# First pair's outputs from direct scores between its blocks; second pair's keys turned on TensorE

## Chip, cores and metric

One core of a Trainium2 chip. The metric is device time in microseconds (us), the median of three runs. Names of engines as in the profile: PE (TensorE, with PEld for its weight loads), DVE (VectorE), ACT (ScalarE), POOL (GpSimd), SP (SyncE, which issues the DMAs).

## What is computed

Attention with a decaying state, then two gated layers, in float32 and better (weights come as 64-bit numbers). Cut to what matters:

```python
# r, k, v, w: (4, 8, 768, 48); u: (8, 48)
for t in range(S):
    cur = einsum("bhd,bhe->bhde", u[None] * kt, vt)
    y[:, :, t] = einsum("bhd,bhde->bhe", rt, state + cur)
    state = wt[:, :, :, None] * state + einsum("bhd,bhe->bhde", kt, vt)
x = y.transpose(0, 2, 1, 3).reshape(3072, 384)
x = (1 / (1 + exp(-(x @ w_gate))) * (x @ w_val)) @ w_out         # 384 -> 1536 -> 384
h = x @ w_in                                                     # 384 -> 2048 -> 384
out = (h * tanh(log1p(exp(h)))) @ w_out2
```

## The kernel before

The sequence of 768 is cut into 24 blocks of 32 (`C`), taken in 12 pairs; block `e` (0 or 1) of pair `p` is block `2p+e`. One pair gives 256 rows of x, and each pair goes through the same stages.

*Attention of a pair.* `fine` builds the scores inside small squares of a block from products of r and k rows (`pt`, `blk`, mostly POOL) that DVE sums into `A`. `coarse` transposes r, k, w on DVE into `RD`, `KD`, `WD`, scales `RD`, and makes the scores further from the diagonal on PE (`scores`, tile `lp`, one bank per block). DVE transposes `A` into `X`, and twelve small copies per block merge `lp` into `X` (`merge`, L715). `keys` multiplies the keys by decays on POOL, transposes them on DVE (`flip`, tile `KT`, L782), and ACT copies the parts into `KK` (`gather`, L797; eight copies for a pair below 2). `states_apart` multiplies `KK` by v on PE (`kp`, L902), and DVE adds the product to the decayed state (`s`, L913, L915; the decay is L833). `rows_out` multiplies `X` by v and `RD` by the old state on PE (`yp`, L948); ACT and DVE copy the sums as a high and a low fp16 half (`xs`, L976, L979). For the first two pairs `turn` transposes `xs` on PE against an identity (`xp`, L1000), and ACT and DVE copy one half each to `xt`; later pairs use transposing DMAs. For pairs 0 and 1 the order is: outputs of block 0, state behind block 0, outputs of block 1, state behind block 1. So block 1 of pair 0 waits for the state behind block 0.

*The first layer.* `gate` runs 24 rounds of nine products for each pair (`gv`, L1072) from `xt` and the two weights `wgs`, `wvs`; ACT takes the sigmoid, DVE the product (L1088), and both split it into `gt`. `out1` multiplies by `wos` (`o`, L1140). Beside the gates of pair 0 the weights are decoded from 64-bit numbers: SP loads a chunk into one of three raw buffers, ACT makes two parts (`word`, `low`), DVE joins them (L350, L444), ACT casts the high half, and DVE or POOL subtracts the low one (L364, L457). The second layer (`h`, L1250; `o`, L1365) follows, and its products come after the attention.

*What sets the order.* Every step is a task with the engines it may go to, a cost, and keys that it reads and writes. `Plan.run` gives each task a due time, counted back from the end, plays the program once with the costs, and issues the instructions in the order that results; a task with two engines goes to the one that the play finds free. So a change of a cost or of an order in the code moves instructions on all engines. An engine then works through its own list in order. `FIRST` is the pair of gate steps before which the two halves of the next pair's tail (`tail1`, `tail2`) are entered; `MERGE` says which blocks ACT merges; for pairs below `TURNED`, `turn_keys` transposes the keys on PE instead of DVE; none did.

Of the kernel before, what the change touches and what calls it, by code (L numbers as in the profile page):

```python
# [8 lines left out]
F32 = mybir.dt.float32  # L9
# [4 lines left out]
ALU = mybir.AluOpType  # L14
# [28 lines left out]
YPOS = (4, 7)  # L43
FIRST = (9, 11)
LATE = 3
# [6 lines left out]
APART = 2  # L52
TURNED = 0
KBANKS = ((('pg', 0), ('pg', 1)), (('at', 0), ('at', 2)))
# [8 lines left out]
WORDS = 256  # L63
MERGE = lambda p, e: e == 0 or p == 0
CROWD = 208
# [149 lines left out]
def mixer_moe_kernel(  # L215
# [266 lines left out]
    late = {}  # L482
    yps = {}
    kps = {}
    xss = {}
# [155 lines left out]
    def coarse(p, cells):  # L641
# [85 lines left out]
        parts = [(*RD, n) for n in range(3)]  # L727
        attn("pe", BURST, scores, [*parts, KD], banks, burst=space(p), words=256)
        attn("dve", 1.9, flip_a, [*cells], X[0] + X[1])
        for e in range(2):  # L730
            for n in range(4):
                on = {"act": 0.85} if MERGE(p, e) else {"dve": 0.95}
                attn(on, 0, lambda on, e=e, n=n: merge(on, e, n), [banks[e]], [X[e][n]])
        attn({"dve": 0.85, "pool": 1.45}, 0, lambda e: scaled(e, 1, 1, 3, 0), [WD], [(*RD, 1)])

    def turn_keys(p, K):

        banks = KBANKS[p]
        kts = {}

        def sums(_):
            for n in range(2):
                kts[n] = bank_tile(banks[n], [128, 12, 2, HG], F32, f"kt{p}_{n}")
            k = rows(p)[1]
            for d in range(DH):
                for q in range(4):
                    o = 64 * (q // 2) + 8 * (q % 2)
                    pick = eyes[1][:, o : o + 56]
                    pick = bass.AP(
                        pick.tensor, pick.offset, [list(pick.ap[0]), [16, 4], [1, 8]]  # L750
                    )
                    nc.tensor.matmul(
                        kts[d // 12][32 * q : 32 * q + 32, d % 12],
                        k[:, :, d],
                        pick,
                        start=True,
                        stop=True,
                    )

        def put(on, n):  # L760
            out = KK[:, p % 2, :, :, 12 * n : 12 * n + 12]
            src = kts[n].rearrange("p d h x -> p x h d")
            (nc.scalar.copy if on == "act" else nc.vector.tensor_copy)(out=out, in_=src)

        attn("pe", 2.2 * COLD, sums, [K, "eye"], banks, burst=space(p), words=385)
        kk = [("KK", p % 2, q, g, h) for q in range(4) for g in range(2) for h in range(2)]
        for n in range(2):
            attn({"act": 0.55, "dve": 0.5}, 0, lambda on, n=n: put(on, n), [banks[n]], [(k, n) for k in kk])
        attn("none", 0, lambda _: None, [(k, n) for k in kk for n in range(2)], kk, lat=0.0)

    def keys(p):
# [28 lines left out]
        attn("pool", 1.0, lambda e: update(e, 16), [W], [K])  # L800
        if p < TURNED:
            turn_keys(p, K)
            return
# [87 lines left out]
    def states_apart(p, e):  # L891
# [17 lines left out]

        def put(hf):  # L910
            s = ss[j + 1][:, 8 * hf : 8 * hf + 8]
            if j:
                nc.vector.tensor_tensor(out=s, in0=kps[p, e, hf], in1=s, op=ALU.add)  # L913
            else:
                nc.vector.tensor_copy(out=s, in_=kps[p, e, hf])  # L915

# [6 lines left out]
        for hf in range(2):  # L923
            attn("dve", 0.48, lambda _, hf=hf: put(hf), [banks[hf]], S(j + 1)[2 * hf : 2 * hf + 2])

    def rows_out(p, es, banks):
        X = [("X", p % 2, e, n) for e in es for n in range(4)]
        RD = [("RD", p % 2, n) for n in range(2)]
        V = [("v", (2 * p + e) % 3) for e in es]
        old = [k for e in es for k in S(2 * p + e)]  # L930

        def sums(_):
# [5 lines left out]
            for e in es:  # L938
                j = 2 * p + e
                for h in range(4):  # L940
                    for n in range(2 if j else 1):
                        for t in range(2):
                            for b in range(B):
                                g = b // 2 ^ t
                                gs = slice(64 * g, 64 * g + 64)
                                i = b % 2 * H + 4 * t + h
                                x = HG * e + i
                                nc.tensor.matmul(  # L948
                                    yps[j, t][32 * b : 32 * b + 32, h * D : h * D + D],
# [5 lines left out]

        cost = 2.58 if len(es) > 1 else BURST * (COLD if p < 2 else 1.0)
        attn("pe", cost, sums, [*X, *RD, *V, *old], banks, burst=space(p), words=257 if p + es[0] else 129)
        xs = [[("xs", e, t, i) for i in range(2) for e in es] for t in range(2)]

# [30 lines left out]
    def turn(p, e):  # L990
# [10 lines left out]

        def put(on, i):
            if not e and not i:
                new_xt()
            out = xt[p][:, i, :, 128 * e : 128 * e + 128]
            if i:
                nc.vector.tensor_copy(out=out, in_=xps[p, e][:, i])
            else:
                nc.scalar.copy(out=out, in_=xps[p, e][:, i])

# [10 lines left out]
        if p < 2:  # L1021

            (tbank,) = next_at(1) if p < APART else BANKS[2:3]
            attn("pe", 0.6, flip_x, [*reads, "eye"], [tbank], words=13)
            attn("act", 0.48, lambda on: put(on, 0), [tbank, *room], [("xt", p % 2, e, 0)])
            room = [("xt", p % 2, 0, 0)]
            attn("dve", 0.48, lambda on: put(on, 1), [tbank, *room], [("xt", p % 2, e, 1)])
        else:
# [443 lines left out]
    def tail1(p):  # L1472
        coarse(p, cells[p])
        keys(p)
        if p < APART:
            rows_out(p, (0,), next_at(2))
# [7 lines left out]
    def tail2(p):  # L1484
        if p < APART:
            rows_out(p, (1,), next_at(2))
# [145 lines left out]
```

## Time and profile before

| | us |
|---|---|
| median of 3 runs | 929.12 (927.22 to 932.88) |
| profiled execution | 927.52 |
| its span on the core | 925.8 |
| outside the span | 1.7 |
| PE busy in the span | 867.1 (94%) |
| DVE, ACT, POOL busy | 638.7, 496.9, 503.2 |

Times in all rows count from the start of the span of this one execution. "Busy" is time in which an engine has an instruction at work; "idle before" names what the engine waited for.

### The profile page before, as it was taken

What the parts mean: (1) busy time and instruction counts of PE and PEld (TensorE: products, weight loads), DVE (VectorE), ACT (ScalarE), POOL (GpSimd) and SP (SyncE); (2) the same over time, 40 slices, a digit from 0 to 9 for tenths busy, and PEclk for the clock granted to TensorE, in tenths of its full rate; (3) what the DMA queues carried; (4) which work ended last, traced back from release to release, by engine and by line L of the source; (5) the groups of instructions that cost most, each with busy time, mean ns of one, the idle gap of its engine ahead of it and who ended that gap; (6) DMA issues with size and microseconds to landing.
All of it is one profiled execution on the core that took longest, in us unless ns stands there. A gap on an engine that the chain in (4) does not pass through costs nothing.

```text
span 925.8 us, 29360 instructions
## 1 busy us (share of the span) xinstructions
PE 867.1 (94%) x12808; PEld 700.4 (76%) x12808; DVE 638.7 (69%) x1094; ACT 496.9 (54%) x1144; POOL 503.2 (54%) x557
## 2 busy tenths in 40 slices
PE   0378899999999999999999999999999999999998
PEld 0266778878888888888888885567677676776788
DVE  7799898965775758666778877775555655556541
ACT  2888855352634525252538777665555655556540
POOL 6987874728475564748372385553433434334320
PEclk9999999999999999999999999999999999999999
DMA  9284725142313222323214910010200102000000
GB/s 339 94 283 157 259 69 128 38 89 81 96 43 100 84 61 77 92 60 79 57 49 150 285 58 13 12 35 2 69 1 26 45 1 70 1 18 18 2 35 35
DMA packets 55313, 74.26 MB, mean 80 GB/s; under 512 B 19600, under 2 KB 36496, under 8 KB 55056
## 3 DMA queue, kind: packets, MB, share of 16 engines
q1 hardware_dynamic: 55184, 72.38, 26.1%
q8 instruction: 100, 1.64, 0.8%
q14 instruction: 29, 0.24, 0.1%
HBM read 58.99 MB, written 9.44 MB: 74 GB/s over the span
## 4 chain that ended last, share of the span: by engine, by line
PE 83%; DVE 7%; ACT 4%; DMA 2%; POOL 2%; issue 1%; SPq 0%; DVEq 0%; ACTq 0%; POOLq 0%
PE gv L1072 27%; PE h L1250 20%; PE o L1365 18%; PE o L1140 13%; PE yp L948 3%; ACT KK L797 2%; PE kp L856 2%; ACT X L715 1%; DMA xt<-xs 1%; PE lp L694 1%; DVE KD L663 1%; DVE A L565 1%; POOL blk L545 1%; DVE RD L659 1%; DVE KT L782 1%
## 5 line engine op out<-in xcount | busy, mean ns | idle before, releaser
L1250 PE MATMUL h<-x,wis 128*128 128x512 f16 x864 | 199.9, 379 | 0.0
L1072 PE MATMUL gv<-xt,wgs 128*128 128x256 f16 x1296 | 167.2, 275 | 4.7 <-DMA xt<-xs 3.2
L1284 POOL TENSOR_TENSOR sum<-e 128x256 f32<-128x256 f32 x96 | 71.8, 748 | 179.9 <-ACT e L1261 179.9
L1072 PE MATMUL gv<-xt,wvs 128*128 128x256 f16 x1296 | 167.3, 276 | 2.1 <-POOL s L833 2.0
L1140 PE MATMUL o<-gt,wos 128*128 128x256 f16 x1296 | 165.8, 274 | 0.6 <-DVE wos L364 0.5
L1250 PEld LDWEIGHTS <-wis 128*128 128x128 f16 x864 | 83.5, 98 | 82.9
L545 POOL TENSOR_TENSOR blk<-blk 128x384 f32<-128x384 f32 (+4 forms) x150 | 125.7, 851 | 35.0 <-DMA blk<-rkw 18.7
L1072 PEld LDWEIGHTS <-wgs 128*128 128x128 f16 x1296 | 126.2, 99 | 21.8 <-DMA xt<-xs 2.1
L1140 PEld LDWEIGHTS <-wos 128*128 128x128 f16 x1296 | 126.4, 98 | 19.8 <-DVE wos L364 0.8
L1072 PEld LDWEIGHTS <-wvs 128*128 128x128 f16 x1296 | 126.6, 99 | 19.2 <-issue 1.4
L545 POOL TENSOR_TENSOR pt<-blk 128x384 f32<-128x384 f32 x93 | 106.9, 1173 | 38.1 <-DMA blk<-rkw 35.7
L1261 ACT ACTIVATE e<-h 128x512 f32<-128x512 f32 x96 | 57.3, 597 | 85.9 <-PE h L1250 85.0
L1088 DVE SCALAR_TENSOR_TENSOR gv<-gv,sig 128x512 f32<-128x512 f32 x72 | 50.5, 702 | 55.0 <-PE gv L1072 27.9
L1083 ACT ACTIVATE sig<-gv 128x512 f32<-128x512 f32 x72 | 42.0, 596 | 83.7 <-PE gv L1072 83.4
L1100 ACT CAST gt<-gv 128x512 f16<-128x512 f32 x72 | 42.1, 585 | 68.2 <-DVE gv L1088 68.1
L797 ACT COPY KK<-KT 32x192 f32<-32x192 f32 (+1 forms) x176 | 64.0, 363 | 22.4 <-DVE KT L782 19.8
L1365 PE MATMUL o<-wps,gt 128*128 128x192 f16 x612 | 74.0, 246 | 0.0
L833 POOL TENSOR_TENSOR s<-s,WD 128x384 f32<-128x384 f32 x38 | 34.5, 918 | 51.5 <-DVE s L885 33.8
L1303 DVE SCALAR_TENSOR_TENSOR gt<-e,gt 128x256 f16<-128x256 f32 x41 | 27.5, 682 | 49.6 <-ACT gt L1298 49.6
L1365 PE MATMUL o<-wps,wgs 128*128 128x192 f16 x498 | 59.4, 246 | 0.0
L1365 PE MATMUL o<-wps,wos 128*128 128x192 f16 x456 | 57.1, 246 | 0.0
L1103 DVE TENSOR_TENSOR gt<-gv,gt 128x512 f16<-128x512 f32 x72 | 49.3, 685 | 10.2 <-ACT gt L1100 9.6
(111 smaller groups left out, 1461.6 us busy)
## 6 DMA issues: line engine op xcount, KB each, us to landing
v<-vt SPq DMA_DIRECT2D x24, 480.0 KB, 4.4
blk<-rkw SPq DMA_DIRECT2D x22, 384.0 KB, 3.3
raw_wi<-wi SPq DMA_DIRECT2D x8, 768.0 KB, 4.8
raw_wp<-wo SPq DMA_DIRECT2D x8, 768.0 KB, 5.6
blk<-rkw SPq DMA_DIRECT2D x11, 512.0 KB, 4.1
raw_wg<-wg SPq DMA_DIRECT2D x6, 768.0 KB, 6.9
raw_wv<-wv SPq DMA_DIRECT2D x6, 768.0 KB, 5.4
raw_wo<-wo SPq DMA_DIRECT2D x6, 768.0 KB, 4.2
```

The source lines that it names most:

```text
L545: engines[e].tensor_tensor(out=pv, in0=a, in1=b, op=ALU.mult)
L797: nc.scalar.copy(out=to, in_=own)
L1072: nc.tensor.matmul(gps[p, i, o][:, h], w[:, a, kc, fs], xt[p][:, c, kc, :], start=(n == 0), stop=(n == 3 * KC - 1),)
L1083: nc.scalar.activation(out=sgs[p, i], in_=gps[p, i, 0], func=AF.Sigmoid, scale=1.0 / (SW * SX))
L1088: nc.vector.scalar_tensor_tensor(out=gps[p, i, 1], in0=gps[p, i, 1], scalar=SG / (SW * SX), in1=sgs.pop((p, i)), op0=ALU.mult, op1=ALU.mult,)
L1100: nc.scalar.copy(out=gt[p][:, 0, 2 * i : 2 * i + 2], in_=gps[p, i, 1])
L1103: nc.vector.tensor_tensor(out=gt[p][:, 1, 2 * i : 2 * i + 2], in0=gps[p, i, 1], in1=gt[p][:, 0, 2 * i : 2 * i + 2], op=ALU.subtract,)
L1140: nc.tensor.matmul(ops[p, c][:, :NT], wos[:, a, f, cs], gt[p][:, g, f, :], start=(f == 0 and n == 0), stop=(f == NF1 - 1 and n == 2),)
L1250: nc.tensor.matmul(hps[r, f], w2["wi"][:, a, kc, fs], x2[r][:, c, kc, :], start=(n == 0), stop=(n == 3 * KC - 1),)
L1261: nc.scalar.activation(out=es[r, f], in_=hps[r, f], func=AF.Mish, scale=ih)
L1284: engines[e].tensor_tensor(out=sums[0][:, n - 1], in0=a(), in1=b(), op=op)
L1365: nc.tensor.matmul(ops2[h, first], home(slots[r, i, name])[:, c, tsl], w2["wp"][:, a, w, i, :], start=(new and n == 0), stop=(n == 3 * NF2 ...
```

## The change

For pair 0 block 1 no longer needs the state behind block 0. `cross` multiplies the keys of block 0, scaled by decays into a spare tile (the tile `RD` of pair 1), by the scaled r of block 1: 32 small products on PE (`lpc`), copied by ACT. `rows_out` then makes both blocks' outputs at once, with these scores times v of block 0 in the place of state times r, and both states of pair 0 are made behind them. The merges of pair 0's block 1 may go to DVE. The keys of pair 1 (and of no other) are turned by PE: 96 products with columns of the identity, and two copies into `KK`. One copy of `turn` takes both halves, and either ACT or DVE does it. Pair 0's first state copy may go to ACT. The tails of pairs 1 to 3 are entered at gate steps 8 and 10 instead of 9 and 11.

```diff
-FIRST = (9, 11)
+FIRST = (8, 10)
...
-TURNED = 0
+TURNED = (1,)
...
-MERGE = lambda p, e: e == 0 or p == 0
+MERGE = lambda p, e: e == 0
...
-        attn("pe", BURST, scores, [*parts, KD], banks, burst=space(p), words=256)
+        attn("pe", BURST, scores, [*parts, KD], [*banks, ("lp", p)], burst=space(p), words=256)
         attn("dve", 1.9, flip_a, [*cells], X[0] + X[1])
         for e in range(2):
             for n in range(4):
                 on = {"act": 0.85} if MERGE(p, e) else {"dve": 0.95}
                 attn(on, 0, lambda on, e=e, n=n: merge(on, e, n), [banks[e]], [X[e][n]])
         attn({"dve": 0.85, "pool": 1.45}, 0, lambda e: scaled(e, 1, 1, 3, 0), [WD], [(*RD, 1)])
+        if p == 0:
+            cross([KD, WD], [(*RD, 0), (*RD, 1)])
+
+    def cross(kw, R):
+        spare = {}
+        T = [("RD", 1, n) for n in range(3)]
+        bank = ("pg", 2)
+
+        def new(_):
+            t = ap.tile([128, BH, RC], F32, tag="RD1", name="cross")
+            t = t.rearrange("p x t -> p (x t)")
+            spare["k"] = t[:, : HG * C].rearrange("p (x t) -> p x t", t=C)
+            spare["x"] = t[:, HG * C : HG * C + 8 * C].rearrange("p (x t) -> p x t", t=C)
+
+        def last(_):
+            nc.scalar.copy(out=spare["k"][:, :, 24:], in_=kd[0][:, :HG, 24:])
+
+        def scaled(e, lo, hi, w, own=False):
+            src = spare["k"] if own else kd[0]
+            engines[e].tensor_tensor(
+                out=spare["k"][:, :, lo:hi],
+                in0=src[:, :HG, lo:hi],
+                in1=wd[0][:, w, :HG].unsqueeze(2).to_broadcast([128, HG, hi - lo]),
+                op=ALU.mult,
+            )
+
+        def sums(_):
+            spare["p"] = bank_tile(bank, [128, 8, C], F32, "lpc")
+            for i in range(8):
+                for q in range(2):
+                    for g in range(2):
+                        o = 64 * g + 32 * q
+                        x = 8 * q + i
+                        gs = slice(64 * g, 64 * g + 64)
+                        nc.tensor.matmul(
+                            spare["p"][o : o + 32, i],
+                            spare["k"][gs, x],
+                            rd[0][gs, HG + x, :C],
+                            start=True,
+                            stop=True,
+                        )
+
+        def put(_):
+            nc.scalar.copy(out=spare["x"], in_=spare["p"])
+            xcs[0] = spare["x"]
+
+        attn("none", 0, new, [], [*T, "xc"], lat=0.0)
+        attn("act", 0.3, last, ["KD", T[0]], [("kc", 2)])
+        attn({"dve": 0.33, "pool": 0.63}, 0, lambda e: scaled(e, 0, 16, 3), [*kw, T[0]], [("kc", 0)])
+        attn({"dve": 0.2, "pool": 0.35}, 0, lambda e: scaled(e, 0, 8, 2, True), [*kw, T[0]], [("kc", 0)])
+        attn({"dve": 0.2, "pool": 0.35}, 0, lambda e: scaled(e, 16, 24, 6), [*kw, T[0]], [("kc", 1)])
+        attn("pe", 1.0, sums, [T[0], *[("kc", n) for n in range(3)], *R], [bank], burst=space(0), words=65)
+        attn("act", 0.4, put, [bank, T[0]], ["xc"])
...
-        attn("pe", 2.2 * COLD, sums, [K, "eye"], banks, burst=space(p), words=385)
+        attn("pe", 2.2 * COLD, sums, [K, "eye", ("lp", p)], banks, burst=space(p), words=385)
...
-        if p < TURNED:
+        if p in TURNED:
...
-        def put(hf):
+        def put(on, hf):
             s = ss[j + 1][:, 8 * hf : 8 * hf + 8]
             if j:
                 nc.vector.tensor_tensor(out=s, in0=kps[p, e, hf], in1=s, op=ALU.add)
             else:
-                nc.vector.tensor_copy(out=s, in_=kps[p, e, hf])
+                (nc.scalar.copy if on == "act" else nc.vector.tensor_copy)(out=s, in_=kps[p, e, hf])
...
-            attn("dve", 0.48, lambda _, hf=hf: put(hf), [banks[hf]], S(j + 1)[2 * hf : 2 * hf + 2])
+            both = {"dve": 0.48} if j else {"act": 0.5, "dve": 0.48}
+            attn(both, 0, lambda on, hf=hf: put(on, hf), [banks[hf]], S(j + 1)[2 * hf : 2 * hf + 2])
 
     def rows_out(p, es, banks):
         X = [("X", p % 2, e, n) for e in es for n in range(4)]
         RD = [("RD", p % 2, n) for n in range(2)]
         V = [("v", (2 * p + e) % 3) for e in es]
-        old = [k for e in es for k in S(2 * p + e)]
+        old = [k for e in es for k in S(2 * p + e)] if p else ["xc", ("RD", 1, 0)]
...
+                                if n and not p:
+                                    gs = slice(64 * g + 32 * (i // 8), 64 * g + 32 * (i // 8) + 32)
+                                    nc.tensor.matmul(
+                                        yps[j, t][32 * b : 32 * b + 32, h * D : h * D + D],
+                                        xcs[0][gs, i % 8],
+                                        vs[0][gs, i, :],
+                                        start=False,
+                                        stop=True,
+                                    )
+                                    continue
...
-        attn("pe", cost, sums, [*X, *RD, *V, *old], banks, burst=space(p), words=257 if p + es[0] else 129)
+        attn("pe", cost, sums, [*X, *RD, *V, *old], banks, burst=space(p), words=257 if p else 193)
...
-        def put(on, i):
-            if not e and not i:
+        def put(on):
+            if not e:
                 new_xt()
-            out = xt[p][:, i, :, 128 * e : 128 * e + 128]
-            if i:
-                nc.vector.tensor_copy(out=out, in_=xps[p, e][:, i])
-            else:
-                nc.scalar.copy(out=out, in_=xps[p, e][:, i])
+            move = nc.scalar.copy if on == "act" else nc.vector.tensor_copy
+            move(out=xt[p][:, :, :, 128 * e : 128 * e + 128], in_=xps[p, e])
...
-            attn("act", 0.48, lambda on: put(on, 0), [tbank, *room], [("xt", p % 2, e, 0)])
-            room = [("xt", p % 2, 0, 0)]
-            attn("dve", 0.48, lambda on: put(on, 1), [tbank, *room], [("xt", p % 2, e, 1)])
+            new = [("xt", p % 2, e, i) for i in range(2)]
+            attn({"act": 0.83, "dve": 0.6}, 0, put, [tbank, *room], new)
...
     def tail1(p):
         coarse(p, cells[p])
         keys(p)
-        if p < APART:
+        if p == 0:
+            rows_out(p, (0, 1), next_at(2))
+            for e in range(2):
+                states_apart(p, e)
+                load_v(3 + e)
+        elif p < APART:
             rows_out(p, (0,), next_at(2))
             states_apart(p, 0)
             load_v(2 * p + 3)
...
     def tail2(p):
-        if p < APART:
+        if p == 0:
+            pass
+        elif p < APART:
             rows_out(p, (1,), next_at(2))
             states_apart(p, 1)
             load_v(2 * p + 4)
```

The planner puts this into another order. On DVE, at pair 0's scores (`blk_95` is pair 0's input, `lp_1` the scores of its block 1), before:

```order
L565 TENSOR_REDUCE A<-pt 128x2x4x4
L782 STREAM_TRANSPOSE KT<-blk_95 128x24x32
L677 TENSOR_TENSOR RD_164<-RD_164,WD_175 128x32x16
L704 STREAM_TRANSPOSE X_192<-A 128x32x32
L677 TENSOR_TENSOR RD_164<-RD_164,WD_175 128x32x24
L444 SCALAR_TENSOR_TENSOR word_wg_138<-word_wg_138,low_wg_132 128x384
```

and in the changed kernel, where "..." stands for nine more copies of `lp_1`:

```order
L566 TENSOR_REDUCE A<-pt 128x2x4x4
L755 TENSOR_TENSOR cross<-KD_171,WD_178 128x16x16
L678 TENSOR_TENSOR RD_166<-RD_166,WD_178 128x32x16
L705 STREAM_TRANSPOSE X_189<-A 128x32x32
L678 TENSOR_TENSOR RD_166<-RD_166,WD_178 128x32x24
L716 COPY X_189<-lp_1_192 24x8x8
L716 COPY X_189<-lp_1_192 16x8x16
L716 COPY X_189<-lp_1_192 8x8x24
...
L836 STREAM_TRANSPOSE KT<-blk_95 128x24x32
L444 SCALAR_TENSOR_TENSOR word_wg_140<-word_wg_140,low_wg_134 128x384
```

The transpose of the keys has moved from ahead of the scaling to behind the merges, which are new on DVE.

On ACT, from the end of pair 0's merges to the copies of x (`xt`), before:

```order
L715 COPY X_192<-lp_1_195 8x8x24
L976 ACTIVATE xs_103<-yp_0_0_288 128x192
L976 ACTIVATE xs_103<-yp_0_1_289 128x192
L715 COPY X_192<-lp_1_195 24x8x8
L715 COPY X_192<-lp_1_195 16x8x16
L715 COPY X_192<-lp_1_195 8x8x24
L454 CAST wgs<-word_wg_138 128x3x128
L454 CAST wgs<-word_wg_140 128x3x128
L361 CAST wvs<-word_wv_154 128x3x256
L1009 COPY xt_361<-xp_0_350 128x3x128
```

and in the changed kernel:

```order
L716 COPY X_189<-lp_0_191 8x8x24
L779 COPY cross<-lpc 128x256
L851 COPY KK<-KT 32x16x24 x2
L1041 ACTIVATE xs_99<-yp_0_0_325 128x2x192
L1041 ACTIVATE xs_99<-yp_0_1_326 128x2x192
L851 COPY KK<-KT 32x16x24 x6
L1071 COPY xt_466<-xp_0_449 128x6x128
L454 CAST wgs<-word_wg_140 128x3x128
L1071 COPY xt_466<-xp_1_459 128x6x128
L454 CAST wgs<-word_wg_142 128x3x128
```

The eight KK copies, which stood ahead of and between the merges, now stand around the copies of both blocks' outputs, and both copies of x are on ACT.

## Rows read from the trace of the kernel before

**Rows 1.** The page, section 4: shares of the span in the chain that ended last.
```profile
PE 83%; DVE 7%; ACT 4%; DMA 2%; POOL 2%; issue 1%; SPq 0%; DVEq 0%; ACTq 0%; POOLq 0%
```
**Rows 2.** Busy time by stretch: start:end, length, busy time (instructions) of each engine, clock, DMA.
```profile
core 0: us, PE busy (x) PEld busy (x) DVE busy (x) ACT busy (x) POOL busy (x), PEclk, DMA share, GB/s
...
200.00:300.00 100.00, 100.00 (x2064) 88.66 (x2062) 68.89 (x125) 40.05 (x103) 59.58 (x64) 1.00 0.28 76
```
**Rows 3.** Timeline of PE: start, duration, engine, line, operation, count, idle before.
```profile
27.34 1.79 PE L694 MATMUL lp<-RD,KD 64*32 64x48 f32 x128 [27.34 <-DVE RD L677]
...
50.27 0.80 PE L1000 MATMUL xp<-first,xs 128*128 128x128 f16 x6 [3.17 <-DVE xs L979]
...
52.03 1.94 PE L902 MATMUL kp<-v,KK 32*64 32x48 f32 x60 [0.58 <-ACT xt L1009]
...
53.90 2.10 PE L1072 MATMUL gv<-xt,wgs 128*128 128x256 f16 x9
```
**Rows 4.** Busy time of DVE in two stretches: length, busy (instructions), clock, DMA.
```profile
37.61:99.73 62.12, 57.39 (x88) 0.95 0.59 201
99.73:117.05 17.32, 16.62 (x19) 1.00 0.81 255
```
**Rows 5.** Timeline of DVE.
```profile
24.39 2.11 DVE L782 STREAM_TRANSPOSE KT<-blk 128x768 f32<-128x768 f32 x1 [1.13 <-POOL blk L545]
26.29 0.99 DVE L677 TENSOR_TENSOR RD<-RD,WD 128x512 f32<-128x512 f32 x1
27.21 2.00 DVE L704 STREAM_TRANSPOSE X<-A 128x1024 f32<-128x1024 f32 x1
29.19 0.96 DVE L677 TENSOR_TENSOR RD<-RD,WD 128x768 f32<-128x768 f32 x1
...
77.26 3.76 DVE L715 COPY X<-lp 24x64 f32<-24x64 f32 x12
```
**Rows 6.** Timeline of POOL.
```profile
24.32 0.64 POOL L677 TENSOR_TENSOR RD<-RD,WD 128x256 f32<-128x256 f32 x1
...
40.88 3.60 POOL L545 TENSOR_TENSOR blk<-blk 128x384 f32<-128x384 f32 x5
```
**Rows 7.** Timeline of ACT.
```profile
26.54 3.64 ACT L797 COPY KK<-KT 32x384 f32<-32x384 f32 x7 [11.23 <-DVE KT L782]
...
36.71 0.55 ACT L976 ACTIVATE xs<-yp 128x192 f16<-128x192 f32 x2
...
39.76 0.47 ACT L1009 COPY xt<-xp 128x384 f16<-128x384 f16 x1
```
**Rows 8.** Groups of DVE, 37.61 to 99.8 us: shapes, count, busy us, mean ns, idle before.
```profile
L1088 DVE SCALAR_TENSOR_TENSOR gv<-gv,sig 128x512 f32<-128x512 f32 x6 | 4.2, 703 | 0.5 <-PE gv L1072 0.5
L663 DVE STREAM_TRANSPOSE KD<-blk 128x1024 f32<-128x1024 f32 x2 | 4.0, 2008 | 0.0
...
L350 DVE SCALAR_TENSOR_TENSOR word_wo<-word_wo,low_wo 128x768 uint32<-128x768 uint32 x3 | 3.7, 1238 | 1.9 <-ACT word_wo L306 1.9
...
L364 DVE TENSOR_TENSOR wvs<-word_wv,wvs 128x768 f16<-128x768 f32 x2 | 3.4, 1700 | 0.2 <-ACT wvs L361 0.2
...
L979 DVE SCALAR_TENSOR_TENSOR xs<-yp,xs 128x192 f16<-128x192 f32 x7 | 2.2, 348 | 0.7 <-ACT xs L976 0.7
...
L782 DVE STREAM_TRANSPOSE KT<-blk 128x768 f32<-128x768 f32 x1 | 2.1, 2105 | 0.0
```
**Rows 9.** Timelines of POOL and DVE: a subtraction and a join that meet.
```profile
104.40 1.65 POOL L364 TENSOR_TENSOR wos<-word_wo,wos 128x768 f16<-128x768 f32 x1
...
104.64 2.23 DVE L350 SCALAR_TENSOR_TENSOR word_wo<-word_wo,low_wo 128x768 uint32<-128x768 uint32 x1 [0.70 <-ACT word_wo L306]
```
**Rows 10.** Busy time of PE in three stretches, with the granted clock.
```profile
77.00:81.50 4.50, 2.11 (x128) 1.00 0.61 242
81.50:97.00 15.50, 12.52 (x273) 0.84 0.48 165
...
125.00:133.00 8.00, 6.62 (x152) 0.79 0.06 19
```

More of the change, by code (lines that the diff above doesn't have):

```diff
@@ L483, in mixer_moe_kernel @@
     yps = {}
+    xcs = {}
     kps = {}
```

## Prediction

> **What bounds the kernel now.** I read the page's chain first, then the stretches of TensorE, then the timelines of the first 130 us, engine by engine. The chain goes through TensorE for 83% of the span, and through VectorE (DVE), ScalarE (ACT) and GpSimd (POOL) for nearly all the rest [rows 1]. From 200 us on TensorE has no idle time [rows 2], so an edit counts only by how much sooner it brings TensorE to that state. The first gate product starts at 53.90 [rows 3]; until then TensorE waits for attention of pair 0. Between 37.6 and 99.7 DVE is busy for 57.39 of 62.12 us [rows 4]: there the gates run, but weights are decoded and pair 1's attention is made beside them, all through DVE. So two things bound the opening: the chain to 53.90, and behind it DVE's sum. The change shortens the first by much and the second by less.
>
> **The chain to the first gate, step by step.** Times below are for the changed kernel unless said otherwise; what stands ahead of 23.2 is untouched.
>
> 1. Before, DVE turned the keys (KT, 24.39) ahead of the scaling of RD that the scores wait for (26.29), then X (27.21 to 29.19) [rows 5]. Now KT stands behind the merges. DVE's new multiply into the cross tile (128x256) is not in the trace; it lies between 0 and the 0.99 of the 128x512 row, I take 0.5, and it is free, since RD has to wait for POOL's scaling, which ends at 24.96 [rows 6]. RD then runs 25.0 to 25.9, X to 27.9, the second RD to 28.8. The scores (128 passes, 1.79 [rows 3]) run 26.0 to 27.8.
> 2. The merges of block 0 stay on ACT, those of block 1 go to DVE: twelve copies took DVE 3.76 [rows 5], so 28.8 to 32.6. ACT's twelve start at 28.0 and end by 31.8 even at that rate. Before, ACT did 24, and all stood behind seven KK copies that began at 26.54 and took 3.64 [rows 7].
> 3. The 32 cross products wait for the second RD. They are 64 passes: at the scores' rate 0.9, at kp's rate (60 passes in 1.94 [rows 3]) 2.1; so they end between 29.7 and 30.9 and are hidden by the merges either way. The copy out (128x256 on ACT) is bounded by 0 and the 0.47 of a 128x384 copy [rows 7]; I take 0.4, 31.8 to 32.2, hidden by DVE's merges too.
> 4. The output products of both blocks (96) need the last merge at 32.6; the 64 of block 1 are 128 passes, 1.8 by the scores' row: 34.4. But on ACT two KK copies now stand ahead of the copies that read these outputs, and they wait for KT, which DVE runs 32.6 to 34.7. So ACT does KK 34.8 to 35.8 (0.52 each [rows 7]), then the two high halves (each twice as wide as before; the two old ones took 0.55 [rows 7], so between 0.55 and 1.1, I take 0.9) to 36.7. DVE's low half follows by 37.3.
> 5. Two transposes of 0.80 each [rows 3] end at 38.9. ACT is then in its six other KK copies until 39.9, and copies x out twice with a cast between. A 768-wide copy lies between one and two of the 0.47 row [rows 7]; taken at 0.75, the second ends at 41.8. TensorE's state products wait for the bank that this copy frees, and take 1.94 [rows 3]: the first gate starts at 43.7 to 43.8, **10.1 us earlier**. With the ends of all these bounds it is 42.5 to 45.
>
> **What of that is given back.** The gates need weights, and these come no sooner: the loads wait for raw buffers that ACT and DVE free, and ACT now does KK and the x copies ahead of them. I therefore count DVE from the end of pair 0's low halves (37.6 before, 37.3 now) to the last copy of pair 1's x, which releases the second round of gates (99.73 before). In this stretch the listing of the changed kernel has one KD, one KT and one wvs subtraction less, one join of wo more, and some five short ones less (one s, one gv, two xs, one WD). By their means [rows 8] that is -2.0 -2.1 -1.7 +1.2, and -2.5 for five between 0.35 and 0.70 each: 57.4 becomes 50.3. Idle time was 4.7. Now there is some 1.7 while the cast of the first weights waits behind KK on ACT, and up to 3.5 at pair 1's first RD transpose: its row products on POOL, five that began at 40.88 [rows 6], come about 1.9 later (two cross scalings at 0.4, half of the 0.64 row's width each, and one 128x384 product taken from DVE at about 1.0). With 2 for the casts and copies that stalled DVE before as well, I take 7, between 4 and 10. The end is 37.3 + 50.3 + 7 = 94.6: of the 10.1, **5.1 are left**.
>
> [...]
>
> The turned keys of pair 1 are part of this count: 96 products and two ACT copies replace DVE's KT and eight KK copies. On TensorE 192 passes cost 2.7 at the scores' rate and 6.2 at kp's; I take the 2.7, since the scores too stream short rows from many small weights back to back. They stand between gates that wait for weights; ACT's two copies (768 wide, 0.5 to 0.94 each) replace 4.2 of KK. If that cover is gone, TensorE pays the 2.7 in full.
>
> After 99.73 the third pair's X transpose followed in 17.3 us [rows 4]. Now two wos subtractions (3.4) leave DVE for POOL, and a KD and a KT (4.1) come in, so it takes as long; but KT is then done, and before it followed X. The gather of KK for pair 2, which held TensorE at 125 to 129, starts 2 us earlier still. In 125 to 133 TensorE was busy for 6.62 of 8.00, at a granted clock of 0.79 [rows 10], so there is something to gain. Sum: 5.1 + 2 = **7 us**. Everything behind is TensorE alone, so it stays. The span goes from 925.8 to 918.8, the profiled 927.5 to 920.5; the median of the runs is 1.6 above the profiled one, so I expect 922.
>
> **Rivals.**
>
> - *The early start is kept.* If DVE waits less than 4 us between 37 and 95, and the stall at pair 2's states vanishes with the slow products behind it (1.4 idle; 42% of the stretch at half speed, 1.7), the gain is 10 to 12: 918. For it: the chain to 43.7 rests on rows, and DVE's waits before were 4.7. Against it: the two new waits in DVE's queue.
> [...]
> - *Slower.* The turned keys use the bank of pair 1's own scores, so TensorE waits there for ACT's merges, and the next outputs wait for the two KK copies, which stand behind eight other ACT instructions. [...] Against it: the copies come where gates have their weights, and TensorE's time there is not what bounds.
> - *It doesn't do what it says:* that the first gate starts after 50 because something else holds it. [...]
>
> **How the numbers follow.** The forecast (gain 4 to 9) has 0.52, early start kept 0.25, given back 0.18, slower 0.05. A measurement of this kernel tells about 1% from no change, here 9.3 us. Above that lie four fifths of the second case and a little of the first: 0.24 faster. Slower by over 1% is only the far half of the last case and a tail of unknown waits: 0.04. The range runs from just past the kept start (916.5) to a gain of 1 (928).
>
> **What would show it.** Right: the first gate near 43.8; the scores at 26; the low halves of both blocks near 37; the last x copy of pair 1 near 95; no idle TensorE beyond 1 us at the states of pair 2. Wrong: a first gate after 46 (steps 2 to 5); DVE idle for more than 10 or less than 4 between 37 and 95; a stall of 4 us or more before the turned keys, and gate products as slow as the first nine [rows 3] behind it; or TensorE idle after 200, which would undo that the gain stays.

## The result and the profile after

The changed kernel takes 919.49 us (median of 4 runs, 918.40 to 920.51) against 929.33 for the one before on the same chip: ratio 0.9891, 95% interval 0.9868 to 0.9914. The profiled execution took 919.56, its span 917.8, 8.0 less than before. The forecast was 922 with a gain of 7. The number came close; the way to it failed in most steps behind the first gate, and that the sum came out near is luck.

The page's chain of the changed kernel [rows 1]:

```profile
PE 85%; POOL 4%; DVE 4%; ACT 3%; DMA 2%; issue 1%; SPq 0%; DVEq 0%; ACTq 0%; POOLq 0%
```

DVE's share fell from 7% to 4%. The timeline of PE after the change (start, duration, operation, idle before; "..." stands for rows left out):

```profile
25.62 1.79 PE L695 MATMUL lp<-RD,KD 64*32 64x48 f32 x128 [25.62 <-DVE RD L678]
...
38.16 1.44 PE L1065 MATMUL xp<-first,xs 128*128 128x128 f16 x12 [2.22 <-DVE xs L1044]
...
41.95 1.94 PE L956 MATMUL kp<-v,KK 32*64 32x48 f32 x60 [0.64 <-ACT xt L1071]
43.83 2.10 PE L1133 MATMUL gv<-xt,wgs 128*128 128x256 f16 x9
...
69.19 4.51 PE L806 MATMUL kt<-first,blk 128*32 128x32 f32 x192 [2.82 <-ACT X L716]
...
81.18 0.29 PE L1013 MATMUL yp<-s,RD 64*32 64x48 f32 x9 [3.20 <-issue]
...
98.66 1.16 PE L1133 MATMUL gv<-xt,wgs 128*128 128x256 f16 x9
...
125.80 1.85 PE L910 MATMUL kp<-v,KK 32*64 32x48 f32 x128
...
185.21 1.38 PE L695 MATMUL lp<-RD,KD 64*32 64x48 f32 x128
```

The first gate [rows 3] starts at 43.83, where 53.90 stood. Behind it come three things that the prediction had small or not at all: the turned keys (`kt`) take 4.51, PE stands 2.82 ahead of them, until ACT's merges free their bank, and it stands 3.20 in the middle of pair 1's outputs with no releaser ("issue"). Pair 1's gates begin at 98.66. Before, they and pair 2's states stood at:

```profile
100.93 1.16 PE L1072 MATMUL gv<-xt,wgs 128*128 128x256 f16 x9
...
125.70 0.72 PE L856 MATMUL kp<-v,KK 32*64 32x48 f32 x6
...
128.29 1.51 PE L856 MATMUL kp<-v,KK 32*64 32x48 f32 x114 [0.41 <-ACT KK L797]
```

Timelines of DVE and ACT after the change [rows 5, 7]:

```profile
31.02 0.37 ACT L779 COPY cross<-lpc 128x256 f32<-128x256 f32 x1
...
32.31 2.10 DVE L836 STREAM_TRANSPOSE KT<-blk 128x768 f32<-128x768 f32 x1
...
36.88 3.11 ACT L851 COPY KK<-KT 32x384 f32<-32x384 f32 x6
...
37.10 1.01 DVE L1044 SCALAR_TENSOR_TENSOR xs<-yp,xs 128x384 f16<-128x384 f32 x2
...
41.08 0.82 ACT L1071 COPY xt<-xp 128x768 f16<-128x768 f16 x1
...
67.47 1.77 DVE L364 TENSOR_TENSOR wvs<-word_wv,wvs 128x768 f16<-128x768 f32 x1 [0.58 <-ACT wvs L361]
...
86.57 0.56 DVE L1071 COPY xt<-xp 128x768 f16<-128x768 f16 x1 [3.01 <-PE xp L1065]
...
96.98 0.55 DVE L1071 COPY xt<-xp 128x768 f16<-128x768 f16 x1
```

Ahead of 86.57 DVE waits 3.01 for PE's transpose. Busy time by stretch after [rows 2, 4, 10], first with all engines, then DVE alone:

```profile
core 0: us, PE busy (x) PEld busy (x) DVE busy (x) ACT busy (x) POOL busy (x), PEclk, DMA share, GB/s
...
52.00:60.00 8.00, 4.77 (x42) 3.81 (x41) 8.00 (x14) 7.37 (x14) 7.63 (x6) 1.00 0.67 231
...
130.00:160.00 30.00, 28.57 (x607) 25.17 (x606) 26.57 (x45) 12.72 (x36) 16.97 (x19) 1.00 0.40 106
160.00:200.00 40.00, 40.00 (x941) 35.37 (x939) 34.17 (x61) 21.51 (x56) 21.45 (x24) 1.00 0.30 75
...
300.00:400.00 100.00, 99.94 (x1949) 88.58 (x1947) 72.75 (x126) 44.45 (x123) 57.41 (x65) 1.00 0.29 79
...
38.03:97.45 59.42, 51.96 (x79) 0.94 0.65 218
```

The same stretches of the kernel before, which the prediction had not looked at:

```profile
130.00:160.00 30.00, 28.65 (x592) 24.58 (x591) 25.29 (x46) 12.21 (x35) 12.94 (x12) 0.95 0.42 106
160.00:200.00 40.00, 38.20 (x807) 33.49 (x806) 31.03 (x53) 20.76 (x54) 24.15 (x26) 1.00 0.31 66
...
300.00:400.00 100.00, 98.62 (x2045) 87.06 (x2044) 71.57 (x119) 39.08 (x103) 61.93 (x72) 1.00 0.26 73
```

Before, PE was idle for 1.80 at 160 to 200 and for 1.38 at 300 to 400; after, for 0.00 and 0.06.

**Where the time came from.** To see it, I count the products that PE has done by a given time, each at its cost at a granted clock of 1.00 (0.109 us for a gate or o product, since nine follow each other in 0.98, as at 74.63 and 75.61 in the changed kernel; 1.45 for a pair's scores, 1.6 for a block's outputs, 1.12 for 64 state products, 0.08 for a transpose, all by rows of these traces), without the products that make the cross scores (`lpc`) and the turned keys. The lead is this sum minus that of before at the same time (us, good to about 1, since groups are cut and some records are missing; repeats in x1 are taken off):

| by | changed | x1 | x2 | x8 | x11 | x4 | x9 | x12 | x13 |
|---|---|---|---|---|---|---|---|---|---|
| 65 | 6.6 | 5.6 | 6.7 | 6.4 | 6.6 | 5.6 | 7.1 | 6.7 | 6.6 |
| 75 | -0.7 | -2.1 | -2.1 | 1.3 | -1.2 | 1.5 | 0.0 | -0.6 | -1.3 |
| 100 | 1.3 | 0.7 | -3.4 | 3.4 | 0.7 | 6.6 | 3.0 | 3.2 | 0.5 |
| 125 | -0.1 | -0.1 | -8.0 | 3.2 | -0.4 | -0.7 | -0.9 | 2.9 | -0.4 |
| 140 | 3.7 | 2.1 | -5.4 | 7.0 | 2.7 | 2.3 | 2.3 | 6.2 | 3.0 |
| 200 | 6.6 | 4.6 | -4.9 | 9.5 | 5.8 | -0.1 | 1.6 | 6.9 | -0.1 |
| 400 | 8.0 | 5.9 | -3.9 | 11.2 | 7.1 | 0.5 | 1.5 | 7.0 | 0.7 |

Of the 10.1 us by which the first gate starts earlier, 6.6 are there at 65 and none at 75; at 125 the changed kernel stands level with before. The 8.0 are made later: about 4 at pair 2's states, 3 by pair 3's gates, 1 to 2 between 300 and 400.

### The profile page after: what moved, and what is told of

The parts are those of the page before. It is cut to its first block, busy times and chain, and to the rows that moved or that the text cites. A ratio compares the mean times of both kernels' runs of the same rounds, so it can differ in the third digit from the quotient of the medians.

```text
span 917.8 us, 29861 instructions
## 1 busy us (share of the span) xinstructions
PE 866.2 (94%) x13064; PEld 701.3 (76%) x13064; DVE 633.6 (69%) x1098; ACT 490.7 (53%) x1125; POOL 506.4 (55%) x562
## 4 chain that ended last, share of the span: by engine, by line
PE 85%; POOL 4%; DVE 4%; ACT 3%; DMA 2%; issue 1%; SPq 0%; DVEq 0%; ACTq 0%; POOLq 0%
PE gv L1133 27%; PE h L1311 20%; PE o L1426 18%; PE o L1201 14%; PE yp L1013 3%; POOL pt L546 2%; PE kp L910 2%; POOL blk L546 1%; ACT KK L851 1%; ACT X L716 1%; PE lp L695 1%; POOL wos L364 1%; DMA raw_wv<-wv 1%; DVE A L566 1%; PE kt L806 0%
## 5 line engine op out<-in xcount | busy, mean ns | idle before, releaser
L1201 PE MATMUL o<-gt,wos 128*128 128x256 f16 x1296 | 163.5, 273 | 0.0
L546 POOL TENSOR_TENSOR blk<-blk 128x384 f32<-128x384 f32 (+4 forms) x151 | 123.2, 829 | 30.1 <-DMA blk<-rkw 11.9
L887 POOL TENSOR_TENSOR s<-s,WD 128x384 f32<-128x384 f32 x40 | 37.1, 936 | 55.6 <-DVE s L939 35.7
L851 ACT COPY KK<-KT 32x192 f32<-32x192 f32 (+1 forms) x168 | 59.9, 357 | 10.9 <-DVE KT L836 8.5
```

Of the source, the lines that this page charges most:

```text
L546: engines[e].tensor_tensor(out=pv, in0=a, in1=b, op=ALU.mult)
L851: nc.scalar.copy(out=to, in_=own)
L1201: nc.tensor.matmul(ops[p, c][:, :NT], wos[:, a, f, cs], gt[p][:, g, f, :], start=(f == 0 and n == 0), stop=(f == NF1 - 1 and n == 2),)
```

## Experiments

Two theories after the result. T1: the early start is given back before 125 us, because the gates wait for weights and for DVE, and the gain is made behind. T2: it passes through to the end, as the prediction had it. Each time below is the median, with the ratio to before and its interval.

**x1: a later first gate, same order.**

```diff
-            n = 0
+            for _ in range(5 if (p, i, o, h) == (0, 0, 0, 0) else 1):
...
```

> The nine products of the first gate are issued five times over into the same bank (the same sum each time), and nothing else is changed: the order on every engine stays, and everything behind the first gate is held up on TensorE by four extra groups, between 4 us (at the 1.1 of a fast group) and 8.4 us (at the 2.10 of the first group). Theory 1, the early start is given back before 125 us because the gates behind it wait for weights and for DVE anyway: the end moves by 0 to 2 us, and the last x copy of pair 1 stays within 1 us of 97. Theory 2, the early start passes through DVE's queue to the end as the prediction had it: the end moves by 3 us or more, and that copy by as much.

920.17 us, 0.9892 (0.9864 to 0.9920); the span 920.2, 2.4 above the changed kernel's 917.8. The x copy did not move:

```profile
96.96 0.55 DVE L1071 COPY xt<-xp 128x768 f16<-128x768 f16 x1
```

So PE has 3 to 4 us of room before 60, which the 4.77 busy of 8.00 at 52 to 60 shows too, and T2 falls for this part of the early start. The runs put the price at the end between 0 and 2.4.

**x2: turned keys twice, same order.**

```diff
-            for d in range(DH):
+            for d in [*range(DH), *range(DH)]:
```

> The 96 products that turn the keys of pair 1 are issued twice (the second time over the first, same values), so TensorE has one more such block in the same place, 4.5 us by the profile of the changed kernel, and no order changes. If TensorE's time there is covered, as the prediction had it (the gates wait for weights), the end moves by less than 1 us. If it is on the path, the end moves by 3.5 to 4.5 us.

931.87 us, 1.0019 (0.9996 to 1.0042): 12 us for 4.65 of products (7.94 and 1.22, less 4.51). The timeline of PE:

```profile
69.58 7.94 PE L806 MATMUL kt<-first,blk 128*32 128x32 f32 x339 [3.34 <-ACT X L716]
81.06 1.22 PE L806 MATMUL kt<-first,blk 128*32 128x32 f32 x45 [3.55 <-issue]
...
99.91 0.30 PE L1013 MATMUL yp<-s,RD 64*32 64x48 f32 x3 [2.03 <-issue]
```

The busy time of all engines behind it (columns as above):

```profile
100.00:110.00 10.00, 9.73 (x171) 7.66 (x171) 7.87 (x11) 7.66 (x12) 8.33 (x7) 0.55 0.74 251
```

The last x copy of pair 1 came at 103.70, 6.7 later. A second gap of 2.03 was followed by a stretch at a granted clock of 0.55 (100 to 110); the lead fell by 4.6 more there and in the gaps beside it (-3.4 at 100, -8.0 at 125). The end moved by 12, past both outcomes that were expected. PE's time is not covered here.

**x8: half of the turned keys, same order.**

```diff
-            for d in range(DH):
+            for d in range(DH // 2):
```

with both halves of `kts` in one bank.

> Only the first 48 of the 96 products that turn pair 1's keys are made, into one bank, and both copies into KK read that bank (half of pair 1's turned keys are therefore those of other columns). The order of every engine stays. By the profile of the changed kernel this takes 2.25 us off TensorE at 69 to 74 us. Doubling the block cost 12 us where it added 4.5. If the end follows TensorE's time at 70 to 85 us in both directions, it moves by -2 us or more (-6 if by the same factor). If the 4.5 was just covered, and the factor came from what the added time pushed into (the fetch gap, slow clock, the rows for pair 3), it moves by less than 1 us.

918.63 us, 0.9874 (0.9846 to 0.9902), span 915.4. PE and DVE:

```profile
69.25 2.37 PE L805 MATMUL kt<-first,blk 128*32 128x32 f32 x96 [2.65 <-ACT X L716]
...
91.56 0.24 PE L1012 MATMUL yp<-s,RD 64*32 64x48 f32 x3 [2.19 <-issue]
...
94.83 0.56 DVE L1070 COPY xt<-xp 128x768 f16<-128x768 f16 x1 [0.90 <-PE xp L1064]
```

2.14 less PE time brings the x copy 2.15 earlier, and the span 2.4. The medians differ by only 0.9, within the spread of four runs each: pair 1's x does follow PE one to one; whether the end does, by 0.9 or by 2.4, four runs don't settle. The factor of x2 holds in one direction only.

**x11: the same load on DVE instead, same order.**

```diff
+            nc.vector.transpose(out=KT.rearrange("p b d -> p d b"), in_=k.rearrange("p t d -> p d t"))
             for d in range(DH):
```

> The changed kernel with one more transpose of pair 1's keys on DVE (128x768 into KT, read by nobody), put where the turned keys are issued; nothing else moves on any engine. It gives DVE back the 2.1 us that the turned keys had taken from it. If DVE's queue sets the pace between 50 and 100 us, the last x copy of pair 1 (96.98) comes 1.5 to 2.5 us later and the end moves by +1.5 to +4 us. If DVE has room there (it waits 3.0 for the last transposed x and 2.9 for a part of wo), the end moves by less than 1 us.

920.40 us, 0.9912 (0.9899 to 0.9925), span 918.5 (+0.7).

```profile
69.15 2.13 DVE L799 STREAM_TRANSPOSE KT<-blk 128x768 f32<-128x768 f32 x1
...
97.35 0.55 DVE L1072 COPY xt<-xp 128x768 f16<-128x768 f16 x1
```

2.13 more on DVE delay the x copy by 0.37, where 2.14 on PE moved it by 2.15. So in the changed kernel PE, not DVE's queue, sets pair 1's x (in x11 DVE still waits 3.01 for PE's transpose ahead of the other copy): T1 is right that the start is given back, and wrong that a full DVE takes it. That weights take a part of it is below.

**x7: pair 3's r and k loaded later.**

```diff
+            if p == 3 and i < 2:
+                held.append(lambda: nc.sync.dma_start(out=blk[p][:, cs], in_=rkw[p, :, cs]))
+                return
...
+                    nc.scalar.copy(out=blk[3][:, :1], in_=xss[1][:, 0, 0, :1])
+                    for go in held:
+                        go()
```

> The loads of pair 3's r and k (four issues on SP at 72 to 79 us) are held until the high half of pair 1's block 0 is cast, by one tiny ACT copy into their tile, so that they no longer run at 77 to 81 us. If the 3.2 us for which TensorE stood in the middle of pair 1's output products (no releaser in the trace, DMA near full share) come from its instructions being fetched behind these loads, that gap falls below 1.2 us. If it has another cause, it stays at 2.5 to 3.5 us. Theory 1 (what is won before 100 us is given back): the end moves by 0 to -1 us. Theory 2 (it passes through): -2 to -3 us. A later arrival of pair 3's r and k can cost up to 1 us in either.

919.55 us, 0.9884 (0.9858 to 0.9909).

```profile
80.44 0.29 PE L1017 MATMUL yp<-s,RD 64*32 64x48 f32 x9 [2.10 <-issue]
```

The gap fell from 3.20 to 2.10, between what the two theories said, and the end did not move. So the loads don't make the gap, and that they lengthen it rests on this one trace; what makes it is below.

**x4, x3, x6: parts of the change, in orders that the planner lays anew.**

```diff
-TURNED = (1,)
+TURNED = ()
```

> The change without the turned keys: DVE transposes the keys of pair 1 and gathers them in narrow copies again, as for pair 2; the cross, the early outputs, the merges and FIRST (8, 10) stay, and the planner lays the order anew. Theory 1 (DVE's queue is full in 50 to 100 us, and the cross's start is given back there): without the turned keys DVE has about 4 us more there, the gate of pair 1 that follows its x comes 2 to 4 us later than 98.7, and the end is 3 to 5 us later than the changed kernel's, 922 to 925. Theory 2 (TensorE pays the turned keys, 4.5 and a wait of 2.8): the end is 0 to 4 us earlier than the changed kernel's, 916 to 919.

933.43 us, 1.0038 (1.0018 to 1.0058), 14 above the changed kernel: past T1's 922 to 925.

```profile
71.05 1.48 PE L1133 MATMUL gv<-xt,wvs 128*128 128x256 f16 x12 [3.18 <-POOL wvs L364]
...
123.91 3.70 PE L1133 MATMUL gv<-xt,wgs 128*128 128x256 f16 x18 [4.83 <-DVE gt L1164]
```

This one keeps the early start, 6.6 ahead at 100, and loses it at 105 to 125, when DVE, with the second KT and twelve merges between, holds the gates up for 4.83. In x3 the tails enter at 9 and 11:

```diff
-FIRST = (8, 10)
+FIRST = (9, 11)
```

> The change with the tails of pairs 1 to 3 entered at gate steps 9 and 11 as before; cross and turned keys stay, and the planner lays the order anew. The first gate stays at 43.8. If the 8 us come from the order behind 100 us that the earlier entry gives (pair 2's states without a stall, no wait for pair 3's x), they go: 923 to 929. If cross and turned keys carry them, the end stays within 1.5 us of 919.5.

932.57 us, 1.0028 (1.0005 to 1.0051), past the 923 to 929 that were expected if FIRST carried the gain. The waits of PE list a stop at the scores of a later pair, between 200 and 450:

```profile
PE lp L695 <- POOL RD L678: 2.8, 1, 2.8
```

And x6 has the kernel before with the turned keys alone (and the scores ahead of them in the order):

```diff
-TURNED = 0
+TURNED = (1,)
...
```

> The kernel before with the turned keys of pair 1 alone (and the order of scores ahead of them); no cross, entry at steps 9 and 11, first gate at 53.9. The turned keys take a transpose and eight narrow copies from DVE and ACT and give TensorE 4.5 us and a wait. Theory A, DVE's queue bounds 50 to 125 us and TensorE has room there: 923 to 927, 2 to 6 us faster than before. Theory B, the turned keys are paid by the early start, and without it they are paid by the end: 931 to 936.

938.99 us, 1.0081 (1.0052 to 1.0110): theory B, and 3 more. Its waits of PE from 44 us on:

```profile
PE yp L948 <- issue: 4.6, 2, 3.6
```

Of the 4.6, 3.57 stand at 519.56, and x4 has such a stop of 2.74 at 512.31, x2 one of 1.24 at 513.47; the kernel before and the changed one have none there. So a part of these times is not made in the first 125 us at all.

The turned keys alone (x6), the cross with the turned keys (x3) and the cross with the earlier entry (x4) are not faster than before; all three together are 10 us faster. The cross alone, the entry alone and the entry with the turned keys were not run. Before that is read as one part needing the other, the next four runs ask what an order alone is worth.

**x9: the turned keys in a free bank, order laid anew.**

```diff
-KBANKS = ((('pg', 0), ('pg', 1)), (('at', 0), ('at', 2)))
+KBANKS = ((('pg', 0), ('pg', 1)), (("at",2),("pg",3)))
```

> The turned keys of pair 1 use another bank in the place of the one that pair 1's scores hold, so they don't wait for ACT's merges (2.82 us of idle TensorE before them); the planner lays the order anew. If that wait is lost time on the path, the end moves by -2 to -3 us or more. If TensorE would only wait for the next weights instead (DVE's subtraction of wvs ended at 69.24, the turned keys began at 69.19), the end stays within 1.5 us, apart from what a new order does by itself, which x4 shows can be several us either way.

927.79 us, 0.9970 (0.9951 to 0.9989): 8 later, where 2 to 3 earlier or no change had been expected. The 2.82 are gone, others come:

```profile
67.57 2.68 PE L806 MATMUL kt<-first,blk 128*32 128x32 f32 x96
...
74.91 0.31 PE L1013 MATMUL yp<-v,X 64*32 64x48 f32 x14 [2.11 <-ACT KK L817]
...
124.01 3.58 PE L1133 MATMUL gv<-xt,wgs 128*128 128x256 f16 x18 [3.73 <-DVE gt L1164]
```

The lead is 3.0 at 100 and lost by 125, at the same place as in x4.

**x12, x13, x14: one cost in the planner's play, work unchanged.** x12:

```diff
-        attn("pe", 2.2 * COLD, sums, [K, "eye", ("lp", p)], ...
+        attn("pe", 4.51, sums, [K, "eye", ("lp", p)], ...
```

> The changed kernel with one number of the planner made true: the turned keys cost 4.51 us (as measured) instead of 4.18 in its play. The work is the same; the order differs from pair 1's o products on. Theory O, what the change gains behind 100 us is the order that its particular costs happened to give, and neighbouring orders scatter by several us (x9 changed one bank, took away 2.82 of waiting and was 8 slower): this one ends 3 to 10 us later than the changed kernel, up to the level of before. Theory W, the gain comes from the work saved and moved: within 2 us of 919.5.

x13, and x14 on the kernel before:

```diff
-        attn("dve", 1.9, flip_a, [*cells], X[0] + X[1])
+        attn("dve", 1.98, flip_a, [*cells], X[0] + X[1])
```

> The changed kernel with another number of the planner made true: DVE's transpose of X costs 1.98 us (as measured) instead of 1.9. The work is the same, and TensorE's order is the same up to the gates of pair 3. Theory O: the end lies several us off 919.5, but less than where the order differs from pair 1 on (x12): +1 to +6. Theory W: within 2 us.

> The kernel before with the same number changed (X's transpose 1.98 instead of 1.9). The work is the same. Theory O: the end lies 2 to 8 us off that of before, later if that order was as well chosen as the changed kernel's, on either side if not. Theory W: within 2 us of before.

x12: 920.97 us, 0.9926 (0.9913 to 0.9939), as theory W had it by its time; against its own runs of before it gained 7 where the changed kernel gained 10, and the two intervals just touch. x13: 925.65, 0.9969 (0.9957 to 0.9982), as theory O had it. x14: 928.73, 1.0001 (0.9987 to 1.0015), no change, as theory W had it; its order on TensorE differs from that of before from 160 us on. In x13 TensorE's order is that of the changed kernel up to the first gate of pair 2, at 148 us (the expectation named pair 3's), and its lead is alike up to 140. Then (timeline of PE):

```profile
150.76 0.82 PE L1133 MATMUL gv<-xt,wgs 128*128 128x256 f16 x6 [2.16 <-DMA xt<-xs]
189.74 1.48 PE L695 MATMUL lp<-RD,KD 64*32 64x48 f32 x128 [2.32 <-POOL RD L678]
```

and in the busy time of all engines:

```profile
160.00:200.00 40.00, 37.68 (x791) 32.73 (x790) 30.58 (x53) 21.85 (x57) 25.30 (x27) 0.96 0.31 79
```

Pair 4's scores wait 2.32 for RD on POOL and start 4.5 later than the 185.21 of the changed kernel. The same work in a neighbouring order costs 0 to 6 us by the medians. Against before on the same chip the changed work gained 10, 7 and 3 in the three orders that were run (the changed kernel, x12, x13): each is faster than before, and how much of the 10 is the work and how much this order stays open. The x4, x3, x6 and x9 results too mix the value of a part with that of an order, and what each of the three parts is worth alone stays open. No run beat the changed kernel beyond its interval; x8, 0.9 below, lacks half of the keys.

## Why the prediction came out right, and where its working failed

- **Steps 1 to 5, first gate at 43.7 to 43.8: right.** It was 43.83. Scores at 25.62 (26.0), copy of the cross 0.37 (0.4), second x copy ending at 41.90 (41.8), state products 1.94 (1.94). The outputs behind the last merge took 3.6 instead of 1.8, and the low halves, in two instructions, ended at 38.11 instead of 37.3; the next copies had to wait for ACT's KK until 39.99 anyway.
- **DVE's count from 37.3 to 94.6, "5.1 us are left": the step that failed.** Its terms were close: from the low halves to the end of the x copy, 38.03 to 97.45, DVE was busy for 51.96 (50.3) and idle for 7.46 (7, between 4 and 10). But the copy ended at 97.45 instead of 94.6 and pair 1's gate came at 98.66 after 100.93, so 2.3 were left, and the lead in products was 1.3 at 100. The step that failed is the count of DVE's queue as the bound: x11 moved the copy by 0.37 for 2.13 on DVE, x8 by 2.15 for 2.14 on PE. What the wvs subtraction on POOL saved or cost was not tested by itself.
- **"TensorE's time there is not what bounds", 2.7 for the turned keys: wrong twice.** They took 4.51, inside the bounds of 2.7 to 6.2 but not at the end that I chose, behind a wait of 2.82; together 7.3, and the lead fell by 7.3 between 65 and 75. A slow clock did not make the 4.51: a pass took 22.5 ns at a granted clock of 0.50 (80 passes from 69.2 to 71) and 22.7 at 1.00 (66 from 72 to 73.5). And the wait is not all the keys' own: the gate behind them, at 73.64, needs a part of wvs that DVE had ready only at 69.24 (67.47 and 1.77), so by this trace most of the 2.82 would have stood without them, as x4, which has no turned keys, stands 3.18 for wvs at 71.05; that was not run in the same order. x9 took the wait away and ended later. The rival "slower" had the keys' mechanism, the wait for the bank. The granted clock was no lower than before: 0.91 over 70 to 100, against 0.89. What it missed is that the order behind 125 us would win the time back; and in x4, which doesn't pay for the turned keys, the lead was lost later, at 105 to 125.
- **"Starts 2 us earlier still" at pair 2's states: not earlier, and worth more than 2.** They start at 125.80, no earlier than the 125.70 of before, but run 1.85 without a stop, and the products behind them at a granted clock of 1.00 (125 to 133), where [rows 10] showed 0.79 (0.50 from 130 to 132). The lead grew by about 4 from 125 to 140.
- **"Everything behind is TensorE alone, so it stays": wrong.** I read [rows 2] of one stretch, 200 to 300, and concluded for all. The neighbours had 1.80 and 1.38 of idle time; these went, and the lead grew there by some 4 of the 8 (from 3.7 at 140 to 6.6 at 200 and 8.0 at 400). x13 loses them again with the same work.

So the 7 of the forecast is luck: it was 5.1 and 2 on paper, and by the lead 0 up to 125, 4 to 140 and 4 behind. Of the other cases, "early start kept" had about the size (10 to 12 against 9.8), "given back", at 0.18, the outcome up to 125, though not by DVE's queue (x11). The span gained 8.0, the medians 9.8: the profiled execution of before was 1.8 faster than its median, that of after at it. The ratio lies on the border of 1% on which the chances were split.

In the changed trace a join on DVE that began at 88.97, 0.04 after a wvs subtraction on POOL (1.65), took 2.42, where the one at 87.04, with POOL idle, took 0.95 (timelines of DVE and POOL); [rows 9] show such a meeting at 2.23. What lengthens the join was not tested.

```profile
87.04 0.95 DVE L350 SCALAR_TENSOR_TENSOR word_wv<-word_wv,low_wv 128x768 uint32<-128x768 uint32 x1
...
88.93 1.65 POOL L364 TENSOR_TENSOR wvs<-word_wv,wvs 128x768 f16<-128x768 f32 x1 [7.00 <-ACT wvs L361]
...
88.97 2.42 DVE L350 SCALAR_TENSOR_TENSOR word_wo<-word_wo,low_wo 128x768 uint32<-128x768 uint32 x1
```

x11 shows that 2.13 more on DVE there moved the end by 0.7 to 0.9.

## What to carry to other kernels

An earlier start is worth only what the next bound leaves of it: ask which engine pays for the new work, and test it by doubling and halving that work in a frozen order before trusting a count of queues. "No idle time" holds for the stretch that was read; read every stretch. Where a planner lays the order, run one neighbouring order of each kernel before crediting a few us to a change: here the same work scattered by up to 6.

## What the runs showed of the hardware

PE's gaps without a releaser stand at fixed places of its program. Busy time and count of PE from the start to the gap, in the changed kernel, x2, x8 and before:

```profile
0.00:81.13 81.13, 39.27 (x1116) 0.98 0.64 221
```

```profile
0.00:81.01 81.01, 38.47 (x1117) 0.96 0.61 207
```

```profile
0.00:91.51 91.51, 46.91 (x1244) 1.00 0.67 232
```

```profile
0.00:81.22 81.22, 35.78 (x862) 1.00 0.66 232
```

The gap follows pass 1117 whether that is an output product or, in x2, one of the turned keys; with 96 passes less (x8) it appears one step of 128 further on, 10 us later. The other gaps of x2 up to 150 us stand at 1372, 1500, 1884 and 2267, two or three records short of further steps of 128 from 862. A pass is a weight load and a product (the page counts 13064 of each after, 12808 of each before), so a step is 256 instructions.

The page's DMA queues name what arrives at such a step (packets, MB, share), after and before:

```profile
q8 instruction: 102, 1.67, 0.8%
```

```profile
q8 instruction: 100, 1.64, 0.8%
```

TensorE has 13064 passes after and 12808 before: 102 and 100 times 256 instructions. Each of these packets carries 16,384 bytes. In the traces a packet of this queue lands at 79.76 in the changed kernel, at 79.62 in x2, 90.12 in x8 and 79.92 before, each 1.35 to 1.44 ahead of the product that ends the gap; in all 14 traces each of the 33 gaps of over 0.3 us without a releaser ends 1.25 to 1.58 behind such a packet. So by these traces PE stood there for its own instructions. The gap is 0.79 before, 3.20 after 192 passes of turned keys in 4.5 us and outputs close behind, 2.10 in x7 with fewer loads beside it, where the packet took as long (1.01 against 0.98) but started 0.76 sooner; in x2 the gap of 3.55 lasted 2 us beyond the end of the loads (DMA share 0.00 from 79 to 81). In these four traces a burst of small products thus outran its own instructions, by 0.79 to 3.55. That moving a burst against this grid would save the 3.20 was not tried.
